# A block-sparse attention and MoE kernel with every engine's queue in the planned order

## The chip, the cores and the metric

The kernel runs on one core of a Trainium2 chip. The metric is the device time in microseconds (us) of one execution. A core has five engines with a queue each: TensorE (PE, matmuls), VectorE (DVE), ScalarE (ACT), GpSimd (POOL) and SyncE (SP, which here issues nearly all DMAs). The engines wait for each other by semaphores.

## What is computed

Attention with a block mask for 4 x 8 heads of 768 tokens by 64, then a feed-forward layer over the 3072 tokens, whose rows are the heads' outputs side by side:

```python
def _attn_ref(q, k, v, sampled_blocks):
    ...
    scores = np.where(mask, scores, -1000000000.0)
    scores = scores - np.max(scores, axis=-1, keepdims=True)
    attn = np.exp(scores)
    attn = attn / (np.sum(attn, axis=-1, keepdims=True) + 1e-09)
    return np.matmul(attn, v).astype(np.float32)

def _moe_ref(x, w_in, w_out):
    h = x @ w_in                    # 3072x512 by 512x2048
    ...
    g = np.where(pos, h, np.where(neg, 0.0, (h + beta) ** 2 / (4.0 * beta)))
    return (g @ w_out).astype(np.float32)
```

`mask` keeps the neighbouring blocks of 32, the first and last, and three sampled blocks for each row of blocks.

## The kernel before

**Precision.** Most operands are split into a rounded part (`hi`, type fp32r, cast on ACT in L196) and the remainder (`lo`, subtracted on DVE), and three products of the parts make one full product.

**A head.** q and k are loaded transposed (`qk`), cast on ACT (L196, `qkh`), and their remainder is taken by DVE (L228). DMAs on SP move the parts (L221) to the tiles KA, QA, KB and QB that the products read. Twelve max products (L267, PE) go one by one into the three `pa` banks, and DVE reduces each to a row maximum (L272). The maxima are joined (L276), turned by PE with the identity `idr` (L282, L293) and stored by ACT or DVE (L287, L298) as a row of QA, so that the score products subtract the maximum themselves. Then, for each half of the queries (`hf`) and each of six pieces of the keys: scores (L318, L319), exponential (L323, ACT), its split (L196 and L331), the sum on POOL (L338) and the product with v (L350, L351) into the one `po` bank. v is split by ACT and DVE (L243). Heads 0 to 9 (pairs 0 to 4, `WHOLE`) use unsplit values (L348) with the row sums as another column of v. Heads 0 to 7, the wide stage, use more banks and tiles for the scores.

**End of a half.** L355 (ACT) and L360 (DVE) take the result out of `po`; L373 (DVE) turns the sums, which L378 (PE) adds up. For each pair and half, L384 and L387 (DVE) take reciprocals; L397 sends them to DRAM and L399 spreads them back as `den` over 64 partitions each, both on SP; L402 (DVE) multiplies, L404 and L410 split the result into `x`. In the pairs that use unsplit values the sums themselves come to L387 by two DMAs first (L392 on ACT's queue, L393 on SP's).

**The feed-forward layer** of a batch is worked off while the next batch's heads run, in halves of 16 blocks: L472 to L474 (PE) into the bank `hp`, L478, L481 (ACT) and L484 (DVE) for the activation, its split (L196, L493), then L500 to L502 (PE). Both weight matrices are split in the kernel (conversions, L162 to L180, a chain between ACT and DVE): `moe_w_in` in the wide stage, `moe_w_out` in the next 8 heads, after which the parts of `moe_w_out` go to DRAM and are loaded again block by block (`w`, L456).

**What sets the order.** Each step is entered in a list `plan` with a planned time, by `at(t, fn, *args)`. The unit is a twelfth of a head's period (`PER = 12`). The times come from tables: `P`, `PW` (heads 0 to 7), `PA` (heads 8 to 15) and `PM` (the first half of the layer), where for example `qs` is how long before its head the cast, the moves and L228 are planned, and `vs` the same for v's split. The list is sorted by time and issued:

```python
    plan.sort(key=lambda x: x[0])
    early = [x for x in plan if x[0] < MANUAL]
    with tc.manual_schedule():
        for _, fn, args in early:
            fn(*args)
    for _, fn, args in plan[len(early):]:
        fn(*args)
```

What is issued inside `manual_schedule` stands in each engine's queue in that order. What is issued outside is a wish: the framework places the instructions of each engine by a model of its own of when they can start, with the order of issue as the priority. In the kernel before, `MANUAL` is -999 and the earliest step stands at -99, so `early` is empty. The constants (identity, mask) are planned at `TC = -90`, head 0's cast at -12.9, so in the plan the constants come first but for the first load.

Of the kernel before, what the change touches and what calls it, by code (L numbers as in the profile page):

```python
# [37 lines left out]
def body(ctx, tc, qk_t, v, sampled_blocks, moe_w_in, moe_w_out, ind, cm, negd, ident, fold, out):  # L38
# [521 lines left out]
# [3 lines that stand above are left out]
# [21 lines left out]
DELAY = 3.672  # L584
EARLY = 0
SETS = 2
MANUAL = -999
NHEADS = B * H
NMOE = B
PER = 2 * T  # L590
# [53 lines left out]
```

## Time and profile before

| | before |
|---|---|
| median of 3 runs | 981.25 us (980.53 to 983.28) |
| profiled execution | 980.94 us |
| its span | 979.0 us |
| granted PE clock, mean | 0.995 |
| PE busy | 945.3 us, 4746 matmuls |
| DVE busy | 736.8 us, 1390 instructions |
| ACT busy | 646.3 us, 1326 instructions |
| POOL busy | 251.5 us, 229 instructions |

The span runs from the first to the last instruction of the profiled execution; its time holds 1.9 us more. A row of the timeline reads: start in us, duration in us, engine, line, operation, output <- input, shapes, and in brackets how long the engine had been idle ahead of it and what released it. A row of the groups gives the count, then the busy time in us, the mean of one in ns, then the idle time ahead of the group. A row of a transfer in the chain gives when it was issued and how long until it landed. PEld is the loading of weights into PE.

### The profile page before, as it was taken

To read this page: it belongs to the slowest core of one execution; us is meant where nothing else is said; L and a number is where in the kernel's file an instruction comes from. 1 tells how busy PE (TensorE), PEld (TensorE's weight loads), DVE (VectorE), ACT (ScalarE), POOL (GpSimd) and SP (SyncE) were. 2 spreads that over 40 slices of the span, in tenths; PEclk is the share of its full clock that TensorE was granted. 3 is DMA by queue.
4 is the path that set the end of the run, shared out by engine and by line. 5 is a ranking of instruction groups with operands and counts; after the bars stand their busy time and mean duration, and the time that the engine had idled before them with its cause. 6 is when DMAs were issued, how large, how long until landed. Compare 5 with 4: busy or idle time off the path is not lost.

```text
span 979.0 us, 14671 instructions
## 1 busy us (share of the span) xinstructions
PE 945.3 (97%) x4746; PEld 833.3 (85%) x4746; DVE 736.8 (75%) x1390; ACT 646.3 (66%) x1326; POOL 251.5 (26%) x229
## 2 busy tenths in 40 slices
PE   5898999999899999999999999999999999999998
PEld 3676677888789999998999899999999999899997
DVE  5897988779998888988888888888788885422222
ACT  4686787677677676767677667776767676433433
POOL 1000000013334443433434343433434343000000
PEclk9899999999999999999999999999999999999999
DMA  6756766754364544545556453646445442433442
GB/s 193 227 155 183 200 201 214 259 173 140 129 205 144 146 148 136 178 135 154 158 154 189 118 153 120 198 138 176 137 143 178 126 114 89 154 129 129 161 129 97
DMA packets 56216, 154.44 MB, mean 158 GB/s; under 512 B 9612, under 2 KB 17952, under 8 KB 56140
## 3 DMA queue, kind: packets, MB, share of 16 engines
q1 hardware_dynamic: 56100, 153.48, 52.0%
q8 instruction: 38, 0.62, 0.3%
q14 instruction: 38, 0.31, 0.1%
q10 hardware_dynamic: 40, 0.03, 0.0%
HBM read 100.92 MB, written 14.81 MB: 118 GB/s over the span
## 4 chain that ended last, share of the span: by engine, by line
PE 88%; DVE 5%; ACT 3%; DMA 2%; issue 2%; SPq 0%; ACTq 0%; DVEq 0%
PE oa L500 8%; PE oa L502 8%; PE oa L501 8%; PE hp L472 8%; PE hp L474 8%; PE hp L473 8%; PE pa L267 7%; PE pa L318 5%; PE pa L319 5%; PE po L350 5%; PE po L348 5%; PE po L351 4%; PE oa L348 3%; DVE mc L272 1%; PE oa L318 1%
## 5 line engine op out<-in xcount | busy, mean ns | idle before, releaser
L338 POOL TENSOR_TENSOR acc<-acc,pt 128x384 f32<-128x384 f32 x176 | 202.2, 1149 | 226.2 <-ACT pt L323 190.3
L272 DVE TENSOR_REDUCE mc<-pa 128x1 f32<-128x384 f32 x384 | 202.8, 548 | 24.1 <-PE pa L267 21.0
L196 ACT CAST ph<-pt 128x384 fp32r<-128x384 f32 x264 | 135.7, 514 | 88.2 <-PE po L350 84.5
L331 DVE TENSOR_TENSOR pl<-pt,ph 128x384 fp32r<-128x384 f32 x264 | 166.3, 630 | 35.6 <-ACT ph L196 34.9
L323 ACT ACTIVATE pt<-pa 128x384 f32<-128x384 f32 x288 | 140.6, 489 | 50.8 <-PE pa L319 42.0
L472 PE MATMUL hp<-x,wi 128*128 128x384 f32 x448 | 155.0, 346 | 2.9 <-DVE r L484 2.9
L500 PE MATMUL oa<-w,gh 128*128 128x512 f32 x384 | 153.6, 400 | 0.3 <-ACT gh L196 0.3
L502 PE MATMUL oa<-w,gl 128*128 128x512 f32 x384 | 151.4, 394 | 0.0
L473 PE MATMUL hp<-x,wi 128*128 128x384 f32 x448 | 151.4, 338 | 0.0
L474 PE MATMUL hp<-x,wi 128*128 128x384 f32 x448 | 151.2, 338 | 0.0
L501 PE MATMUL oa<-w,gh 128*128 128x512 f32 x384 | 150.8, 393 | 0.0
L267 PE MATMUL pa<-KA,QA 88*128 88x384 f32 x384 | 138.8, 381 | 5.3 <-DMA QA<-qkh 3.0
L338 POOL TENSOR_TENSOR acc<-pt 128x384 f32<-128x384 f32 x44 | 45.8, 1040 | 349.4 <-ACT pt L323 349.4
L484 DVE SCALAR_TENSOR_TENSOR r<-r,hp 128x384 f32<-128x384 f32 x112 | 61.7, 551 | 74.0 <-ACT r L481 73.6
L493 DVE TENSOR_TENSOR gl<-r,gh 128x384 fp32r<-128x384 f32 x128 | 83.7, 654 | 23.4 <-ACT gh L196 22.9
L478 ACT ACTIVATE r<-hp,half_c 128x384 f32<-128x384 f32 x112 | 65.1, 582 | 53.4 <-PE hp L474 50.3
L318 PE MATMUL pa<-QA,KA 102*128 102x384 f32 x288 | 99.3, 345 | 0.8 <-ACT pt L323 0.4
L319 PE MATMUL pa<-QB,KB 128*128 128x384 f32 x288 | 97.9, 340 | 0.0
L267 PEld LDWEIGHTS pa<-KA,QA 88*128 88x128 f32 x384 | 73.2, 192 | 27.8 <-DVE mc L272 6.7
L350 PE MATMUL po<-ph,vn 128*128 128x384 f32 x264 | 91.5, 347 | 2.3 <-DVE xun L360 1.9
L472 PEld LDWEIGHTS hp<-x,wi 128*128 128x128 f32 x448 | 84.5, 189 | 8.6 <-DVE r L484 4.2
L351 PE MATMUL po<-pl,vn 128*128 128x384 f32 x264 | 88.6, 336 | 0.0
(100 smaller groups left out, 1634.1 us busy)
## 6 DMA issues: line engine op xcount, KB each, us to landing
w<-wo_dram SPq DMA_DIRECT2D x112, 512.0 KB
qk<-in_qk_t_dram SPq DMA_DIRECT2D x32, 384.0 KB
raw<-in_moe_w_in_dram SPq DMA_DIRECT2D x16, 512.0 KB
raw<-in_moe_w_out_dram SPq DMA_DIRECT2D x16, 512.0 KB
wo_dram<-w SPq DMA_DIRECT2D x16, 512.0 KB
lv<-in_v_dram SPq DMA_DIRECT2D x32, 192.0 KB
KA<-qkh SPq DMA_DIRECT2D x32, 192.0 KB
QA<-qkh SPq DMA_DIRECT2D x32, 192.0 KB
```

The lines of the kernel that those rows point to most:

```text
L267: nc.tensor.matmul(out=pm[:, 0:HALF], lhsT=QAi[0:KM, t * 128:(t + 1) * 128], rhs=KAi[0:KM, kh * HALF:(kh + 1) * HALF], start=True, stop=True)
L272: nc.vector.reduce_max(out=st["mc"][:, t, kh:kh + 1], in_=st.pop(("pm", t, kh))[:, 0:HALF], axis=AX.X)
L318: nc.tensor.matmul(out=ps[:, 0:HALF], lhsT=KAi[0:KA, ks], rhs=QAi[0:KA, cs], start=True, stop=False)
L319: nc.tensor.matmul(out=ps[:, 0:HALF], lhsT=st["KB"][:, ks], rhs=st["QB"][:, cs], start=False, stop=True)
L331: (nc.gpsimd if i < 2 * H and c in PL1 else nc.vector).tensor_tensor(out=pl, in0=st["p", c], in1=f(st["ph", c]), op=ALU.subtract)
L338: nc.gpsimd.tensor_tensor(out=st["acc", hf], in0=prev, in1=st["p", c], op=ALU.add)
L472: nc.tensor.matmul(out=hv, lhsT=wi[:, j, 0, fs], rhs=x[:, 0], start=(j == 0), stop=False)
L473: nc.tensor.matmul(out=hv, lhsT=wi[:, j, 0, fs], rhs=x[:, 1], start=False, stop=False)
L474: nc.tensor.matmul(out=hv, lhsT=wi[:, j, 1, fs], rhs=x[:, 0], start=False, stop=(j == NP - 1))
L500: nc.tensor.matmul(out=o, lhsT=gh[:, ts], rhs=w[:, 0], start=(fi == 0), stop=False)
L501: nc.tensor.matmul(out=o, lhsT=gh[:, ts], rhs=w[:, 1], start=False, stop=False)
L502: nc.tensor.matmul(out=o, lhsT=gl[:, ts], rhs=w[:, 0], start=False, stop=(fi == NF - 1))
```

## The change

One constant is changed, so that `early` holds the whole plan:

```diff
@@ -584,7 +584,7 @@
 DELAY = 3.672
 EARLY = 0
 SETS = 2
-MANUAL = -999
+MANUAL = 99999
 NHEADS = B * H
 NMOE = B
 PER = 2 * T
```

Everything is now issued inside `manual_schedule`. The instructions, tiles and transfers are the same; only their order in the queues differs. Three places:

ACT's queue at the start, before and then after. `QA_113` and `QA_114` are the two sets' QA tiles; L124 casts the mask into them, `qkh` is the cast of q and k, L247 copies v.

```order
L196 ACT_TABLE_LOAD
L196 CAST qkh<-qk 128x768
L124 CAST QA_114<-pa 24x384 x2
L247 COPY vn<-lv 128x6x64
L287 ACTIVATE QA_113<-pa 1x384
```

```order
L124 ACT_TABLE_LOAD
L124 CAST QA_114<-pa 24x384 x2
L196 CAST qkh<-qk 128x768
L287 ACTIVATE QA_113<-pa 1x384
L247 COPY vn<-lv 128x6x64
```

The mask's cast moved ahead of head 0's q and k.

DVE's queue in the wide stage, at the end of pair 1's first half, before the max products of head 5. `rc` holds the reciprocals, `den` what comes back, `cva` belongs to the conversions, `mc` takes the maxima. Before:

```order
L387 RECIPROCAL rc_876<-rc_876 24x32
L228 TENSOR_TENSOR qk_833<-qk_833,qkh_907 128x768
L180 TENSOR_TENSOR wi_119<-cva_1100,wi_119 128x512
L180 TENSOR_TENSOR wi_119<-cva_1169,wi_119 128x512
L169 TENSOR_SCALAR cva_1267<-cva_1267 128x512
L170 TENSOR_SCALAR cva_1267<-cva_1267 128x512
L172 SCALAR_TENSOR_TENSOR cva_1267<-raw_1133,cva_1267 128x512
L272 TENSOR_REDUCE mc_973<-pa_974 128x1
...
L272 TENSOR_REDUCE mc_973<-pa_1024 128x1
L402 TENSOR_TENSOR xun_698<-xun_698,den_699 128x384
```

(The line of dots stands for five more L272.) After:

```order
L228 TENSOR_TENSOR qk_832<-qk_832,qkh_906 128x768
L169 TENSOR_SCALAR cva_919<-cva_919 128x512
L170 TENSOR_SCALAR cva_919<-cva_919 128x512
L172 SCALAR_TENSOR_TENSOR cva_919<-raw_786,cva_919 128x512
L174 SCALAR_TENSOR_TENSOR cva_919<-raw_786,cva_919 128x512
L387 RECIPROCAL rc_875<-rc_875 24x32
L180 TENSOR_TENSOR wi_119<-cva_919,wi_119 128x512
L402 TENSOR_TENSOR xun_697<-xun_697,den_698 128x384
L272 TENSOR_REDUCE mc_972<-pa_973 128x1
```

Between L387 and L402 stood seven maxima, L228 and parts of three conversions; now there is one L180, and the maxima follow L402.

DVE's queue in the steady stage, at the end of the second half of an odd head (around 504 us in the profile before). `pl`, `r` and `gl` belong to the splits and the layer's activation. Before:

```order
L373 TENSOR_REDUCE psum_5646<-acc_5791 128x12
L493 TENSOR_TENSOR gl_5929<-r_5903,gh_5923 128x384
L331 TENSOR_TENSOR pl_5949<-pt_5933,ph_5947 128x384
L402 TENSOR_TENSOR xun_5482<-xun_5482,den_5863 128x384
L410 TENSOR_TENSOR x_5993<-xun_5482,x_5993 128x384
L331 TENSOR_TENSOR pl_5975<-pt_5956,ph_5971 128x384
L484 SCALAR_TENSOR_TENSOR r_5973<-r_5973,hp_5935 128x384
L331 TENSOR_TENSOR pl_6012<-pt_5981,ph_6010 128x384
L360 TENSOR_TENSOR xun_5644<-po_5847,otmp_5989 64x384
L243 TENSOR_TENSOR vn_5995<-lv_5861,vn_5995 128x6x64
```

After:

```order
L331 TENSOR_TENSOR pl_5974<-pt_5955,ph_5970 128x384
L484 SCALAR_TENSOR_TENSOR r_5972<-r_5972,hp_5934 128x384
L402 TENSOR_TENSOR xun_5481<-xun_5481,den_5862 128x384
L228 TENSOR_TENSOR qk_5842<-qk_5842,qkh_5962 128x768
L243 TENSOR_TENSOR vn_5994<-lv_5860,vn_5994 128x6x64
L360 TENSOR_TENSOR xun_5643<-po_5846,otmp_5988 64x384
L373 TENSOR_REDUCE psum_5645<-acc_5790 128x12
L331 TENSOR_TENSOR pl_6011<-pt_5980,ph_6009 128x384
```

L402, L228 and L243 moved between L484 and L360; in an even head L228 and L243 do. L373, which stood eight places ahead of L360, now follows it.

## The prediction

> **What bounds the kernel now.** I read the page's totals and chain first, then the engines' busy time by stage, then what TensorE (PE) waits for.
>
> ```profile
> span 979.0 us, 14671 instructions
> PE 945.3 (97%) x4746; PEld 833.3 (85%) x4746; DVE 736.8 (75%) x1390; ACT 646.3 (66%) x1326; POOL 251.5 (26%) x229
> PE 88%; DVE 5%; ACT 3%; DMA 2%; issue 2%; SPq 0%; ACTq 0%; DVEq 0%
> ```
>
> PE is busy 945.3 of 979.0 us and carries 88% of the chain. An order cannot shorten PE's own work, so all that a better order could win is PE's idle time, 33.7 us. The windows (us, then busy and count for PE, PEld, DVE, ACT, POOL, granted clock, DMA share, GB/s) say where that is:
>
> ```profile
> 0.00:25.00 25.00, 13.31 (x45) 9.89 (x46) 14.46 (x34) 10.39 (x19) 3.50 (x9) 1.00 0.67 193
> 25.00:160.00 135.00, 126.95 (x542) 93.64 (x542) 114.74 (x231) 98.07 (x203) 0.00 (x0) 0.96 0.67 193
> 225.00:300.00 75.00, 68.37 (x355) 60.63 (x355) 73.58 (x133) 52.70 (x112) 29.17 (x24) 1.00 0.46 151
> 300.00:840.00 540.00, 537.55 (x2827) 494.82 (x2826) 443.84 (x831) 381.88 (x797) 213.44 (x191) 1.00 0.50 147
> ```
>
> Idle are 11.7 us at the start, 8.05 in the wide stage (heads 0 to 7, here to 160 us), 6.6 between 225 and 300, where VectorE (DVE) is full (73.58 of 75), and only 2.45 in the 540 us of steady state. There PE never stops, and an order can only lose. Three of PE's waits (total, times, longest):
>
> ```profile
> PE pa L122 <- DVE KA L104: 8.7, 1, 8.7
> PE pa L267 <- DMA QA<-qkh: 3.0, 2, 2.1
> PE po L350 <- DVE xun L360: 1.9, 3, 0.9
> ```
>
> The first is the start itself, which holds in any order: nothing runs before the inputs land.
>
> **The change part by part.** No instruction, tile or transfer is added or removed, so the sum has only displaced waits. What matters is an instruction that now stands in its engine's queue ahead of others while it waits. I go by stages.
>
> **A, the start.** ACT now casts head 0's q and k as soon as they land; in the new order this cast stands behind the two mask casts (L124).
>
> ```profile
> 3.88 0.83 ACT L196 CAST qkh<-qk 128x768 fp32r<-128x768 f32 x1 [1.87 <-DMA qk<-in_qk_t_dram]
> 5.32 0.59 SPq L221 DMA_DIRECT2D QA<-qkh  x1
> 8.06 0.56 DVE L104 CAST KA<-raw 38x768 fp32r<-38x768 f32 x1 [2.90 <-DMA raw<-in_ind_dram]
> 8.68 0.83 PE L122 MATMUL pa<-KA,mb 24*24 24x384 f32 x2 [8.68 <-DVE KA L104]
> 10.04 0.21 DVE L103 CAST idr<-pt 128x128 fp32r<-128x128 f32 x1
> 10.93 0.87 ACT L124 CAST QA<-pa 24x384 fp32r<-24x384 f32 x2 [6.22 <-DVE QA L124]
> 11.61 2.93 PE L267 MATMUL pa<-KA,QA 88*128 88x384 f32 x6 [2.10 <-DMA QA<-qkh]
> 5.32 6.16 DMA QA<-qkh
> ```
>
> The mask's six small DVE steps, done now before L104, come behind it: at L103's 0.21 us each 1.3 us, an estimate. L104 ends at 8.62, the mask's matmuls follow at 9.9 and end at about 10.8, L124 ends on ACT about 12.6 (it starts 1.4 us after those matmuls' end now), the cast takes 0.83, its KA move 0.5, so QA's move is issued near 14.0 instead of 5.32. It took 6.16 us among the loads of the start, which puts the first max product (L267) at 20.2, +8.6. If it takes what a small move later takes (1.92 us, rows of part B), it starts at 16, +4.3. I take the middle, +6, and +1 because all twelve max products of head 0 now stand ahead of its first score: **+7 (4 to 10)**.
>
> **B, the wide stage.** Here each pair of heads sends its reciprocals (L387, DVE) through two transfers on SP's queue (L397 out, L399 spread back as `den`) before L402 multiplies by them.
>
> ```profile
> 101.87 0.33 DVE L387 RECIPROCAL rc<-rc 24x32 f32<-24x32 f32 x1
> 102.23 0.32 SPq L397 DMA_DIRECT2D s<-rc  x1
> 104.15 1.11 SPq L399 DMA_DIRECT2D den<-s  x2
> 109.45 0.55 DVE L402 TENSOR_TENSOR xun<-xun,den 128x384 f32<-128x384 f32 x1
> 438.26 0.33 DVE L387 RECIPROCAL rc<-rc 24x32 f32<-24x32 f32 x1
> 445.21 1.08 DVE L402 TENSOR_TENSOR xun<-xun,den 128x384 f32<-128x384 f32 x1 [0.87 <-DMA den<-s]
> ```
>
> The round trip is seen where L402 waits for it: L387 ends at 438.59, L402 is released at 445.21, 6.6 us. At 102.20 to 109.45 it is longer, but there L402 stands behind other work and waits for nothing. So the framework filled the trip: seven maxima (L272) and a conversion stand between L387 and L402. In the planned order one L180 stands there, and the maxima of the next head stand behind L402.
>
> ```profile
> L272 DVE TENSOR_REDUCE mc<-pa 128x1 f32<-128x384 f32 x384 | 202.8, 548 | 24.1 <-PE pa L267 21.0
> L267 PE MATMUL pa<-KA,QA 88*128 88x384 f32 x384 | 138.8, 381 | 5.3 <-DMA QA<-qkh 3.0 <-ACT pt L323 1.2 <-DVE mc L272 1.0
> L180 DVE TENSOR_TENSOR wi<-cva,wi 128x512 fp32r<-128x512 f32 x16 | 11.0, 686 | 4.7 <-ACT wi L196 4.6
> ```
>
> DVE then idles 6.6 - 0.7 = 5.9 us. PE goes on until the three `pa` banks are full: three max products at 0.38 and about as much of scores between them, some 2 us; the fourth max product waits, and in PE's queue everything behind it. That is 3.9 us for the first half of each of pairs 0 to 3. Behind the second half's L402 stand fewer maxima: between 0 and 3.9, I take 2. Pair 4 (heads 8 and 9), where the row also comes in by DMA and less distance is planned, gets 2 for each half. Sum 4 x 3.9 + 4 x 2 + 4 = 27.6. Against it stands what the planned order may win back, at most the 8.05 us that PE idles there now: **+20**. The lower end: L402's rows give L397 1.92 us to land (102.23 to 104.15); if `den` needed only as much behind its two issues, the trip would be 1.92 + 0.55 + 1.92 = 4.4 us, the first halves lose 1.7, the second nothing, pair 4 half, and B is +1. Upper: 3.9 in all eight halves and nothing won back, +35. I take the trip that was measured.
>
> The Trainium skill, in DMA: Bandwidth & Descriptors, section Anatomy of one DMA — SWDGE (gpsimd) path, fits a transfer as about 2.0 us plus its bytes at 436 GB/s. For L397's 3 KB that is 2.0 us, which the 1.92 us here bears out; for `den`'s 96 KB it would be 2.2, a trip of an estimated 4.2 us, and the whole sum would come out near the first rival's 1014. The 6.6 us row speaks against it: `den` shares SP's queue and the DMA engines with other loads.
>
> **C, 225 to 300 us.** DVE is full, and each of the conversions of `moe_w_out` costs it five steps.
>
> ```profile
> L169 DVE TENSOR_SCALAR cva<-cva 128x512 f32<-128x512 f32 x32 | 13.5, 421 | 4.5 <-ACT cva L168 4.1
> L170 DVE TENSOR_SCALAR cva<-cva 128x512 int32<-128x512 int32 x32 | 15.0, 472 | 0.7
> L172 DVE SCALAR_TENSOR_TENSOR cva<-raw,cva 128x512 int32<-128x512 int32 x32 | 22.8, 716 | 0.4
> L174 DVE SCALAR_TENSOR_TENSOR cva<-raw,cva 128x512 int32<-128x512 int32 x32 | 22.6, 707 | 0.3
> ```
>
> With L180 that is 3.0 us. The planned order holds conversions up to ten DVE instructions later than now, so that one to three more fall into the full stretch: 3 to 9 us more DVE work there, less what PE idles today for other reasons. **+4 (0 to 9)**.
>
> **D, steady heads 16 to 31.** On DVE the long L228 (q's and k's remainders) and L243, in odd heads also L402, now stand straight ahead of L360, which frees the one `po` bank that PE's next product needs (L350), and of L373, for which PE waits in L378. Now, the framework has them elsewhere:
>
> ```profile
> L228 DVE TENSOR_TENSOR qk<-qk,qkh 128x768 f32<-128x768 f32 x32 | 34.6, 1081 | 1.3 <-ACT qkh L196 1.2
> 503.21 0.58 ACT L478 ACTIVATE r<-hp,half_c 128x384 f32<-128x384 f32 x1
> 504.61 0.55 DVE L484 SCALAR_TENSOR_TENSOR r<-r,hp 128x384 f32<-128x384 f32 x1 [0.81 <-ACT r L481]
> 505.77 0.56 DVE L360 TENSOR_TENSOR xun<-po,otmp 64x384 f32<-64x384 f32 x1
> 506.25 0.24 PE L378 MATMUL pa<-sel,psum 128*24 128x32 f32 x2
> 506.37 0.56 DVE L243 TENSOR_TENSOR vn<-lv,vn 128x384 fp32r<-128x384 f32 x1
> 476.76 0.56 DVE L484 SCALAR_TENSOR_TENSOR r<-r,hp 128x384 f32<-128x384 f32 x1 [0.95 <-ACT r L481]
> 477.81 0.54 DVE L360 TENSOR_TENSOR xun<-po,otmp 64x384 f32<-64x384 f32 x1
> 478.47 0.38 PE L350 MATMUL po<-ph,vn 128*128 128x384 f32 x1
> ```
>
> Odd head: from L484's 504.61 on, 0.55, L402 0.55, L228 1.08, L243 0.56, L360 0.56, L373 as long as L360, 0.56: 508.47, against L378 at 506.25, 2.2 us late. Of that I take off 0.3, since L484's input can come that much earlier when ACT goes straight on from L478 (ends 503.79; L484 needs a step of about 0.55 between): +1.9. Even head: 476.76 + 0.56 + 1.08 + 0.54 + 0.54 = 479.48 against 478.47, 1.0, less 0.2: +0.8. PE has no slack in this stage to take it. 8 x 1.9 + 8 x 0.8 = **+22**; 12 if half of it finds cover in work that PE has ahead, 30 if heads 10 to 15 show it too.
>
> After the last head (840 us on) DVE is a quarter busy and nothing changes: 0. SP's queue is in planned order too, but its loads of `w` wait for a free buffer as now: 0, and if a move behind one is late, it shows in A or B.
>
> **Sum.** 7 + 20 + 4 + 22 = +53. The profiled run took 980.94 us, 1.9 more than its span, 0.3 below the median of the runs, 981.25. 981 + 53 = **1034 us**. All lower ends together give 981 + 4 + 1 + 0 + 12 = 998, all upper ones 981 + 10 + 35 + 9 + 30 = 1065.
>
> **The rivals.**
> - *The round trips are short, or hidden.* If DVE runs late enough that `den` has landed when L402's turn comes, B is between -8 (all of the 8.05 us won back) and +1, and the time 1006 to 1014. For it: DVE is busy 114.74 of 135 us there and often behind. Against: L402 waits 0.87 us even at 445.21, with much work between.
> - *Faster.* PE's waits of the first 300 us (8.05 in the wide stage, 6.6 between 225 and 300, and about 2 of the start) vanish because PE's and ACT's queues no longer carry out-of-turn work, and nothing new waits: 981 - 16 = 965. It decides if the plan places each L402 at least 6.6 us of DVE work behind its L387; by the order it has 0.7, which speaks against it.
> - *No change.* The framework's order differs in place but not in what PE waits for: 981. For it: PE's own queue is nearly the same in steady state. Against: part D's L228 and L243 now stand in the queue ahead of what PE needs.
> - *Cascade.* Each stall delays the next head's moves on SP, and PE loses 5 us in every half of every wide pair and 3 in every head: above 1066.
>
> **How the numbers follow.** The sum as worked out 0.66, short or hidden trips 0.18, cascade 0.07, faster 0.06, no change 0.03. The range 998 to 1066 holds the first two and leaves out 0.16. About 0.3% (3 us) is what a measurement of this kernel can tell from no change; faster 0.06, same 0.03, slower 0.91.
>
> **What would show it.** A: ACT's first q/k cast starts near 12.6, the first L267 near 16 to 20. B: L402 of pairs 0 to 3 shows 4 to 6 us of DVE idle released by DMA `den`, and PE waits for L272 at L267 of the same length. C: DVE still full between 225 and 300, its work there larger. D: PE's waits for L360 and L373 grow from 1.9 us to about 20 us. I am wrong if L402 finds `den` there, or if PE's loss per steady head stays under 0.5 us.

## The result and the profile after

The changed kernel takes 1128.1 us (median of 4 runs, 1123.2 to 1131.0) against 981.0 before: 1.149 times as long, 95% interval 1.146 to 1.152. The forecast was 1034 (998 to 1066). The direction was right, the size was not: 147 us were lost where 53 were expected. The profiled run took 1123.16 us with a span of 1121.3, so the two traces differ by 142.3 us, and it is this difference that is divided up below.

The page's totals and the chain after:

```profile
span 1121.3 us, 14619 instructions
PE 985.5 (88%) x4746; PEld 858.5 (77%) x4746; DVE 750.3 (67%) x1390; ACT 644.3 (57%) x1326; POOL 255.1 (23%) x229
PE 55%; DVE 7%; ACT 3%; issue 3%; POOL 1%; DMA 0%; DVEq 0%; SPq 0%; ACTq 0%; POOLq 0%
```

There are the same 4746 matmuls; but PE is now busy for 88% of the span, where it was 97%, and besides it is busy 40 us longer. Both need an explanation. The stages are cut at the first max product (L267) of heads 0, 9, 16 and 31, which starts while the head ahead of it is still at work. First come the windows of before, then those of after:

```profile
11.60:156.40 144.80, 135.83 (x570) 100.62 (x570) 121.72 (x245) 104.53 (x215) 0.00 (x0) 0.96 0.68 196
156.40:367.10 210.70, 203.20 (x1027) 177.75 (x1026) 185.21 (x338) 148.48 (x307) 61.38 (x53) 1.00 0.55 173
367.10:788.70 421.60, 419.39 (x2209) 386.31 (x2208) 353.37 (x663) 301.06 (x628) 168.44 (x150) 1.00 0.53 153
```

```profile
18.30:189.00 170.70, 141.40 (x565) 100.59 (x565) 115.22 (x226) 98.89 (x203) 0.00 (x0) 0.95 0.57 158
189.00:464.70 275.70, 223.40 (x1030) 189.72 (x1031) 202.50 (x355) 149.79 (x318) 56.88 (x54) 0.92 0.44 139
464.70:928.70 464.00, 432.79 (x2209) 398.68 (x2208) 355.98 (x662) 302.87 (x628) 175.32 (x151) 0.97 0.44 139
```

Each stage's loss is the difference of the lengths, split into PE's idle time and its longer busy time for the same products:

| stage | lost, us | PE idle | PE busy longer | forecast |
|---|---|---|---|---|
| start, to head 0's first max product | 6.7 | 6.7 | | A: 7 |
| heads 0 to 8 | 25.9 | 20.3 | 5.6 | B: 20 (pair 4's 4 us of it fall behind this cut) |
| heads 9 to 15 | 65.0 | 44.8 | 20.2 | C: 4 |
| heads 16 to 30 | 42.4 | 29.0 | 13.4 | D: 22 |
| the rest | 2.3 | | | 0 |

What PE waited for:

```profile
PE po L350 <- DVE xun L360: 27.1, 19, 5.5
PE pa L378 <- DVE psum L373: 26.1, 13, 3.9
PE pa L267 <- DVE mc L272: 24.7, 15, 3.5
PE pa L267 <- DMA QA<-qkh: 12.2, 7, 7.3
PE pa L122 <- DVE mb L118: 10.2, 1, 10.2
```

The first three rows, 77.9 of the 131 us that PE's waits come to in this view, are waits for DVE on lines that the prediction named; the last row belongs to the start. DVE itself is busy 67% of the span: it is late because of what stands ahead in its queue, not because it is full.

**Where the 40 us of busy time come from.** Short windows around one steady stall, and the product that ends it:

```profile
552.00:554.00 2.00, 2.00 (x11) 1.73 (x10) 1.29 (x4) 1.73 (x5) 0.58 (x1) 1.00 0.84 218
554.00:556.00 2.00, 0.87 (x4) 0.39 (x3) 2.00 (x2) 2.00 (x5) 0.83 (x1) 1.00 0.79 194
556.00:558.00 2.00, 0.56 (x4) 0.54 (x5) 1.96 (x5) 0.12 (x1) 0.99 (x1) 1.00 0.86 288
558.00:560.00 2.00, 2.00 (x10) 2.00 (x9) 1.41 (x4) 1.00 (x2) 0.00 (x0) 0.63 0.53 157
560.00:562.00 2.00, 2.00 (x8) 2.00 (x7) 0.80 (x2) 0.00 (x0) 1.00 (x1) 0.52 0.00 0
562.00:564.00 2.00, 2.00 (x13) 1.86 (x12) 1.54 (x3) 1.53 (x4) 0.00 (x0) 1.00 0.01 2
498.00:500.00 2.00, 2.00 (x8) 2.00 (x7) 1.32 (x3) 0.49 (x1) 1.00 (x1) 0.50 0.59 123
557.44 0.22 PE L378 MATMUL pa<-sel,psum 128*24 128x32 f32 x2 [2.57 <-DVE psum L373]
525.00:550.00 25.00, 23.63 (x126) 21.60 (x126) 20.54 (x39) 15.24 (x33) 9.06 (x9) 1.00 0.40 127
```

PE idles 2.57 us. About 1 us after it restarts, the granted clock (third column from the end) falls to 0.63 and 0.52 in these windows, that is to 0.50 for 3.4 us, so the stall costs another 1.7 us (2.0 x 0.37 + 2.0 x 0.48) when it is over. The last row is the 25 us before, with a stall of 1.37 us in it: there the clock stays at 1.00. In heads 16 to 30 all seven stalls of 2.57 us are followed so, and none of the seven of 1.37 us; but one stall of 1.40 us, at 494.22, is (the row of 498), with a second one of 0.38 us right behind it.

How much of the longer busy time this is can be read from PE's busy time inside the stretches at 0.50. In heads 16 to 30 it is 27.1 us, of which half, 13.6 us, is lost: all of the 13.4. In heads 9 to 15 it is 31.6 us, so 15.8 of the 20.2; in heads 0 to 8 it is 14.7 us against 9.5 before, so 2.6 of the 5.6. The clock makes 32 of the 39 us; where the other 7 come from is not shown. The Trainium skill, TensorE: Matmul & The Clock Gate, section Why this matters for your kernels, advises against PE-idle gaps of more than about 3 us; the trace agrees in kind, but here 2.6 us were enough each time.

### The profile page after: what moved, and what is told of

Read it like the earlier page. It is cut to its first block, busy times and chain, and to the rows that moved or that the text cites. A ratio compares the mean times of both kernels' runs of the same rounds, so it can differ in the third digit from the quotient of the medians.

```text
span 1121.3 us, 14619 instructions
## 1 busy us (share of the span) xinstructions
PE 985.5 (88%) x4746; PEld 858.5 (77%) x4746; DVE 750.3 (67%) x1390; ACT 644.3 (57%) x1326; POOL 255.1 (23%) x229
## 4 chain that ended last, share of the span: by engine, by line
PE 55%; DVE 7%; ACT 3%; issue 3%; POOL 1%; DMA 0%; DVEq 0%; SPq 0%; ACTq 0%; POOLq 0%
PE hp L472 6%; PE hp L474 6%; PE hp L473 6%; PE oa L500 6%; PE oa L502 6%; PE oa L501 6%; PE po L350 4%; PE po L351 3%; PE pa L318 3%; PE pa L267 3%; PE pa L319 3%; DVE qk L228 1%; DVE vn L243 1%; DVE xun L360 1%; ACT pt L323 1%
## 5 line engine op out<-in xcount | busy, mean ns | idle before, releaser
L338 POOL TENSOR_TENSOR acc<-acc,pt 128x384 f32<-128x384 f32 x176 | 205.8, 1169 | 312.5 <-ACT pt L323 310.3
L272 DVE TENSOR_REDUCE mc<-pa 128x1 f32<-128x384 f32 x384 | 202.3, 548 | 61.5 <-PE pa L267 59.7
L323 ACT ACTIVATE pt<-pa 128x384 f32<-128x384 f32 x288 | 139.8, 486 | 169.3 <-PE pa L319 92.6
L331 DVE TENSOR_TENSOR pl<-pt,ph 128x384 fp32r<-128x384 f32 x264 | 174.1, 659 | 85.5 <-ACT ph L196 82.2
L267 PE MATMUL pa<-KA,QA 88*128 88x384 f32 x384 | 151.5, 405 | 41.9 <-DVE mc L272 24.7
L472 PE MATMUL hp<-x,wi 128*128 128x384 f32 x448 | 160.9, 359 | 0.5 <-DVE r L484 0.5
L473 PE MATMUL hp<-x,wi 128*128 128x384 f32 x448 | 156.6, 350 | 1.5 <-DVE x L410 1.5
L474 PE MATMUL hp<-x,wi 128*128 128x384 f32 x448 | 156.8, 350 | 0.0
L267 PEld LDWEIGHTS pa<-KA,QA 88*128 88x128 f32 x384 | 78.5, 205 | 71.7 <-DVE mc L272 36.9
L350 PE MATMUL po<-ph,vn 128*128 128x384 f32 x264 | 95.2, 360 | 28.8 <-DVE xun L360 27.1
L318 PE MATMUL pa<-QA,KA 102*128 102x384 f32 x288 | 102.6, 356 | 10.5 <-DVE QA L298 4.6
L484 DVE SCALAR_TENSOR_TENSOR r<-r,hp 128x384 f32<-128x384 f32 x112 | 61.7, 551 | 71.8 <-ACT r L481 70.4
L319 PE MATMUL pa<-QB,KB 128*128 128x384 f32 x288 | 100.8, 350 | 0.0
L472 PEld LDWEIGHTS hp<-x,wi 128*128 128x128 f32 x448 | 88.9, 198 | 5.4 <-DVE r L484 1.1
L473 PEld LDWEIGHTS hp<-x,wi 128*128 128x128 f32 x448 | 88.5, 198 | 4.0 <-DVE x L410 2.0
```

The lines of the kernel that those rows point to most:

```text
L267: nc.tensor.matmul(out=pm[:, 0:HALF], lhsT=QAi[0:KM, t * 128:(t + 1) * 128], rhs=KAi[0:KM, kh * HALF:(kh + 1) * HALF], start=True, stop=True)
L272: nc.vector.reduce_max(out=st["mc"][:, t, kh:kh + 1], in_=st.pop(("pm", t, kh))[:, 0:HALF], axis=AX.X)
L323: nc.scalar.activation(out=p, in_=st.pop(("ps", c))[:, 0:HALF], func=AF.Exp, scale=SCALE)
L331: (nc.gpsimd if i < 2 * H and c in PL1 else nc.vector).tensor_tensor(out=pl, in0=st["p", c], in1=f(st["ph", c]), op=ALU.subtract)
L338: nc.gpsimd.tensor_tensor(out=st["acc", hf], in0=prev, in1=st["p", c], op=ALU.add)
L350: nc.tensor.matmul(out=po, lhsT=st["vn"][:, c], rhs=st["ph", c], start=(c == 0), stop=False)
```

## The experiments

All are the changed kernel with the edit shown, but for e14 and e15; the times stand against 1128.1 us and, for before, 981 to 983 us in each group of runs. The table gives by how much the first max product of a head comes later than in the trace of before (e13: than in e14); stages are read as differences along a row. Each row is one trace, and a stage that no edit touches differs between them: heads 0 to 8 lose 25.7 to 32.4 us, heads 9 to 15 62.6 to 68.8, heads 16 to 30 39.2 to 42.5. What lies inside these is not read as an effect.

| run | time, us | head 0 | head 9 | head 16 | head 31 | end |
|---|---|---|---|---|---|---|
| changed kernel | 1128.1 | 6.7 | 32.6 | 97.6 | 140.0 | 142.3 |
| e1 planned to time 0 | 987.8 | 6.8 | 2.5 | 2.7 | 2.9 | 3.1 |
| e2 planned to 96 | 1018.8 | 6.7 | 34.4 | 37.8 | 38.7 | 38.7 |
| e3 planned to 192 | 1083.5 | 6.3 | 33.5 | 102.3 | 105.8 | 106.2 |
| e4 steady steps moved | 1110.5 | 6.7 | 34.4 | 100.6 | 127.1 | 130.0 |
| e5 conversions later | 1136.9 | 6.3 | 33.9 | 116.6 | 159.0 | 161.0 |
| e6 lag of heads 8, 9 | 1121.0 | 6.8 | 37.3 | 96.7 | 139.2 | 140.8 |
| e7 L402 later | 1129.1 | 6.4 | 35.3 | 101.9 | 144.3 | 147.5 |
| e8 steady steps apart | 1087.7 | 6.7 | 39.1 | 101.7 | 109.4 | 111.4 |
| e9 ACT and DVE steps apart | 1121.7 | 6.3 | 29.1 | 97.7 | 136.9 | 138.3 |
| e10 conversions apart | 1119.5 | 6.1 | 23.2 | 91.6 | 133.5 | 134.9 |
| e11 first cast first | 1120.4 | 0.1 | 27.7 | 92.6 | 135.1 | 137.4 |
| e12 combined | 1070.8 | 0.5 | 16.4 | 78.8 | 85.0 | 87.9 |
| e13 against e14 | 1091.7 | 6.7 | 32.4 | 70.6 | 112.4 | 115.1 |
| e16 L360 first | 1114.6 | 6.6 | 36.0 | 89.3 | 131.2 | 133.3 |

**Which stage loses.** Three kernels in which the planned order holds only up to a time:

```diff
-MANUAL = 99999
+MANUAL = 0      # e1; 96 in e2, 192 in e3
```

> Only what is planned before time 0 (constants, preparation of head 0 and part of head 1) is in planned order; the framework orders the rest. Stage theory (each stretch of the program makes its own loss): the loss of the start alone, 6.7 us by the shift of head 0's first max product between the two traces, so about 988 us. Rival (the start's loss is made good later, since the framework fills behind it): within 2 us of before, 981 to 983.

> Planned order up to time 96, that is through the wide stage (heads 0 to 7), the framework after that. Stage theory: the shift of head 9's first max product between the two traces, 33 us, so 1011 to 1016 us. Rival (carry-over: later losses are the aftermath of queues upset in the wide stage): well over that, 1050 or more, since the aftermath remains.

> Planned order up to time 192, that is through heads 8 to 15 with the conversions of the second weight matrix, the framework after that. Stage theory: the shift of head 16's first max product, 98 us, so 1075 to 1085 us. Rival (the steady heads lose because the queues come out of the conversions upset): near the changed kernel, 1115 to 1130.

987.8 (ratio 1.006, 1.003 to 1.009), 1018.8 (1.039, 1.036 to 1.041) and 1083.5 us (1.105, 1.101 to 1.109): as the stage theory said, e2 a little above it. Once the framework takes over, little more is lost: in e2 head 31 is 38.7 us late, where head 9 was 34.4 late. Each stage makes its own loss; the carry-over falls. The other rows bear this out from the other side: heads 16 to 30 lose 39 to 42.5 us in every row that leaves them alone, whatever was lost ahead of them. In e1's profiled run (984.0 us, among the shorter of ten from 983.4 to 993.6) about 4 of the start's 6.8 us are won back in the wide stage; the median is 5.8 us above before, so most runs win back less.

**The start.** e11 plans head 0's cast ahead of the constants:

```diff
-        at(pre - G["qs"] - 0.4, hi)
+        at(-91 if i == 0 else pre - G["qs"] - 0.4, hi)
```

> All in planned order, but head 0's cast of q and k is planned ahead of the constants, so that it stands first in ACT's queue. Theory (term A: the cast stands behind the mask's casts): the first max product starts near 12 to 14 us and not at 18.3, and 4 to 7 us are won, 1121 to 1124. Rival (the moves on SP stand behind the constants' loads, or the lost time is made good elsewhere): under 2 us.

1120.4 us, 7.7 less, a little more than expected, and head 0's first max product is where it was before (0.1 us late). So term A's cause is shown: the cast's place behind the mask's casts. The rows of the changed kernel:

```profile
11.47 1.28 ACT L124 ACT_TABLE_LOAD   x1 [11.47 <-DVE QA L124]
12.76 0.84 ACT L124 CAST QA<-pa 24x384 fp32r<-24x384 f32 x2
13.62 0.83 ACT L196 CAST qkh<-qk 128x768 fp32r<-128x768 f32 x1
15.06 0.59 SPq L221 DMA_DIRECT2D QA<-qkh  x1
18.30 2.93 PE L267 MATMUL pa<-KA,QA 88*128 88x384 f32 x6 [7.26 <-DMA QA<-qkh]
```

**The steady heads.** The changed kernel at the end of a half of an even head:

```profile
523.97 0.95 DVE L228 TENSOR_TENSOR qk<-qk,qkh 128x768 f32<-128x768 f32 x1
524.84 1.36 DVE L243 TENSOR_TENSOR vn<-lv,vn 128x384 fp32r<-128x384 f32 x1
526.13 0.54 DVE L360 TENSOR_TENSOR xun<-po,otmp 64x384 f32<-64x384 f32 x1
526.82 0.41 PE L350 MATMUL po<-ph,vn 128*128 128x384 f32 x1 [1.37 <-DVE xun L360]
```

This is the order of term D, and PE stands for it: 1.37 us in each even head and, with L402 ahead as well, 2.57 us in each odd one. The prediction had 0.8 and 1.9. The difference is the length of L228 and L243: they were priced at 1.08 and 0.56 us, 1.64 together, and take 2.31 here and 2.32 in the odd head, while a sum on POOL runs beside them (last section):

```profile
553.87 1.77 DVE L228 TENSOR_TENSOR qk<-qk,qkh 128x768 f32<-128x768 f32 x1
555.57 0.55 DVE L243 TENSOR_TENSOR vn<-lv,vn 128x384 fp32r<-128x384 f32 x1
```

e4 moves these steps just behind L360 and L373; e8 moves them apart, to where DVE idled. The casts, loads and moves that are planned with them move too.

```diff
-P = {... 'qs': 9.647, ... 'vs': 9.131, ... 'xm': 0.774, 'xh': 1.0, ...}
+P = {... 'lo': 0.8, ... 'vs': 8.75, ... 'xm': 1.3, 'xh': 1.5, ...}     # e4; L228 at -qs + lo
+P = {... 'qs': 10.85, ... 'vs': -0.6, ...}   # e8; xm, xh + 0.53 in heads 16 to 31 but for j = 3
```

> All in planned order as in the changed kernel, but for heads 16 to 31 the planned times of L402 (xm 0.774 to 1.3, with its cast xh 1.0 to 1.5), of L228 (0.4 units later) and of v's split L243 (vs 9.131 to 8.75) are moved just behind L360 and L373. Theory (these three stand ahead of what frees PE): PE's waits for L360 and L373 after 465 us (31 us) go, and with them the clock dips behind them; 35 to 45 us faster than the changed kernel, 1083 to 1093. Rival (DVE is late in the steady heads for other reasons, such as L484 waiting for ACT): under 10 us faster, over 1118.

> All in planned order, but for heads 16 to 31: q and k prepared 1.2 units earlier (qs 10.85), v's split only when its head begins (vs -0.6), L402 0.53 units later except in each batch's last pair. So L228, L243 and L402 stand apart from each other and from L360, where DVE idled. Theory (e4 removed the waits for L360 and L373, but moved 2.5 us of DVE work in one piece ahead of L331, L493 and the maxima): 33 to 45 us faster than the changed kernel, 1083 to 1095. Rival (the planned order leaves other waits in the steady heads): no better than e4, 1105 to 1112.

e4 takes 1110.5 us, half of the gain expected: after 465 us PE's waits for L360 and L373 fall from 30.7 to 5.5 us, but DVE then has L360, L373, L402, L228 and L243 in one piece, and 11.9 us of waits for the maxima behind it (L272) appear. e8 takes 1087.7 us, as expected; heads 16 to 30 lose 7.7 us instead of 42.4. In e8 after 465 us little is left of the waits (19.9 us stood in the first row in the changed kernel, 10.8 in the last):

```profile
PE pa L378 <- DVE psum L373: 3.6, 9, 1.1
PE pa L267 <- DVE mc L272: 2.0, 6, 0.3
PE po L350 <- DVE xun L360: 1.9, 3, 0.8
```

So term D's mechanism is shown: three instructions of DVE with the steps tied to them, and where they stand.

**The wide stage.** The changed kernel's wait on a round trip:

```profile
104.44 0.33 DVE L387 RECIPROCAL rc<-rc 24x32 f32<-24x32 f32 x1
109.53 0.56 DVE L402 TENSOR_TENSOR xun<-xun,den 128x384 f32<-128x384 f32 x1 [3.62 <-DMA den<-s]
```

```diff
-XLATE = 2.0
+XLATE = 4.0
```

> All in planned order, but L402 and what follows it are planned 2 units later in pairs 0 to 2 (XLATE 2 to 4), behind maxima of the next head. Theory (term B: the round trip of the reciprocals stands ahead of the maxima): DVE's waits for den in the wide stage (10.6 us in 4 waits) go and most of PE's waits for L272 (19.2 us): 10 to 18 us faster than the changed kernel, 1110 to 1118. Rival (in the wide stage the conversions of the first matrix hold up DVE, which waits 13.0 us at L169 for ACT): under 5 us faster.

1129.1 us: nothing, as the rival had it. No wait of DVE for `den` is left in the wide stage, yet PE's wait for the maxima there, 19.2 us in the changed kernel, stays (first row, of e7), and other waits of DVE have grown in its place (second and third, 13.0 and 9.4 us in the changed kernel):

```profile
PE pa L267 <- DVE mc L272: 20.3, 13, 2.8
DVE cva L169 <- ACT cva L168: 16.5, 12, 4.8
DVE qk L228 <- ACT qkh L196: 13.2, 5, 3.6
```

Term B was about right in size, by luck, and wrong in its cause, or at least had one of several. e9 and e10 take the next of these away: the ACT and DVE steps of a conversion are planned 0.8 units apart (e9), and its DVE steps also 0.4 apart from each other (e10).

```diff
-            at(t, bits)
-            at(t + P["cs"], split)
+            at(t - 0.8, bits)            # L168 alone
+            at(t, bits1)                 # L169, L170
+            at(t + 0.4, bits2)           # L172; + 0 in e9
+            at(t + 0.8, bits3)           # L174; + 0 in e9
+            at(t + P["cs"], split)       # the cast
+            at(t + P["cs"] + 0.8, split_lo)
```

> All in planned order; the conversions' ACT and DVE steps, which share one planned time in the changed kernel, are planned apart: L168 (ACT) 0.8 units before the four DVE steps, the cast L196 0.8 units before L180. Theory (a DVE step planned at the same time as the ACT step it needs stands at the head of DVE's queue and waits, with all behind it): DVE's waits at L169 for L168 (23.3 us) and at L180 for the cast (8.7 us) mostly go, PE's waits for L272 and L360 before 465 us fall, 12 to 30 us faster than the changed kernel, 1098 to 1116. Rival (the length of the DVE block and not its wait is what PE sees): under 6 us faster.

> As e9, and the four DVE steps of a conversion are planned 0.4 units apart (L169 with L170, L172, L174) and no longer back to back, so that other DVE work can stand between. Theory of the wait alone: within 4 us of e9. Rival (the block of 2.3 us ahead of L360 or a maximum is the loss): 8 to 25 us faster than e9.

1121.7 and 1119.5 us. e9's 6.4 us less are under what its theory asked for, although DVE's waits at L169 before 470 us fell from 23.3 to 3.7 us: this wait of DVE for ACT cost PE little. e10 is 2.2 us below e9, within the 4 us in which the two were to agree. By its trace the gain of e10, 9.4 us at head 9 (23.2 against 32.6), lies in the wide stage; heads 9 to 15 lose as much as ever.

**Heads 9 to 15**, where nearly all of the error lies. The changed kernel at the end of a half:

```profile
297.04 1.37 DVE L172 SCALAR_TENSOR_TENSOR cva<-raw,cva 128x512 int32<-128x512 int32 x1
298.44 0.69 DVE L174 SCALAR_TENSOR_TENSOR cva<-raw,cva 128x512 int32<-128x512 int32 x1
299.06 0.57 DVE L373 TRANSPOSE_TENSOR_REDUCE psum<-acc 128x12 f32<-128x384 f32 x1
299.55 0.51 DVE L360 TENSOR_TENSOR xun<-po,otmp 64x384 f32<-64x384 f32 x1
300.20 0.66 PE L350 MATMUL po<-ph,vn 128*128 128x384 f32 x1 [4.18 <-DVE xun L360]
```

The conversion's steps stand ahead of L373 and L360, as L228 and L243 do later. The plan has it so wherever both occur: the conversions of the second matrix come every 3 units at -0.02 (modulo 3), L373 at 0.04, L360 at 0.31. But these conversions are planned from 98.98 to 143.98, so they fill heads 8 to 11 and not eight heads, and heads 8 and 9 have no L360 and L373. It is so at the ends of three halves, and each is a long stall of PE: 4.18 us in the rows above, and

```profile
323.00 0.66 PE L350 MATMUL po<-ph,vn 128*128 128x384 f32 x1 [5.47 <-DVE xun L360]
345.13 0.30 PE L378 MATMUL pa<-sel,psum 128*24 128x32 f32 x2 [3.86 <-DVE psum L373]
```

In all that is 13.5 of the 44.8 us by which PE's idle time grew in this stage. e5 moves the conversions behind (and the loads of both matrices one unit later); e6 lets ACT stop waiting for the three `pt` buffers in heads 8 and 9.

```diff
-P = {... 'cl': 9.0, ... 'co': 5.196, ...}
+P = {... 'cl': 8.0, ... 'co': 4.796, ...}                                   # e5
-... {**P, **PA} if i < 2 * H else P
+... {**P, **PA, **({"lag": 2.9} if whole else {})} if i < 2 * H else P      # e6
```

> All in planned order, but the conversions of the second weight matrix are planned 0.4 units later (co 5.196 to 4.796), so that their five DVE steps (3 us) stand behind L373 and L360 and not straight ahead of them, and their loads one unit later (cl 9 to 8), so that SP's queue does not stand at a load until the buffer is free. Theory (position of the conversions): of PE's waits for L360 and L373 between 189 and 465 us, 21.4 us, most go, with the clock dips behind them: 20 to 35 us faster than the changed kernel, 1093 to 1108. Rival (the stretch is simply full of DVE work, as the prediction had it): the waits reappear elsewhere, under 10 us faster.

> All in planned order, but in heads 8 and 9 (unsplit values, three buffers for the exponentials) the values are planned 2.9 instead of 3.5 units behind their scores, so that an exponential no longer stands in ACT's queue ahead of the product that frees its buffer. Theory: ACT's waits of L323 for L348 (37.8 us in 21 waits between 189 and 465 us) hold back what stands behind them on ACT, and the 24 us that heads 8 and 9 lost come largely from it: 12 to 22 us faster than the changed kernel, 1106 to 1116. Rival (ACT's idle is off the path and the loss is SP's and DVE's): within 4 us of it.

e5 takes 1136.9 us (ratio to before 1.157, 1.155 to 1.159): slower, and the expected gain did not come. PE's waits for L360 and L373 between 189 and 472 us did fall from 21.4 to 8.9 us, but other losses rose by more: 43.7 us are lost between the first max products of heads 9 and 11, where the changed kernel loses 25.7. Its ACT and DVE rows point to the reason (37.8 and 3.0 us stood here in the changed kernel):

```profile
ACT pt L323 <- PE po L348: 53.9, 22, 6.0
DVE w L180 <- ACT w L196: 33.9, 11, 6.4
```

A reading of these rows, not tested by itself: the cast of a conversion now stands in ACT's queue behind an exponential that waits for its buffer, L180 waits for the cast at the head of DVE's queue, and the maxima wait behind L180. e6 takes 1121.0 us, 7.1 less where 12 to 22 were expected: ACT's waits of 37.8 us for L348 are gone, but ACT's waits for L319 rise from 48 to 72 us. In its trace heads 9 to 15 lose 5.6 us less and heads 0 to 8 4.7 us more. e5 and e6 together were not run, apart from what e12 joins. Whether the conversions matter at all was told by leaving out their steps L169 to L174 for the second matrix, in both orders; such a kernel does not compute the layer:

```diff
-            nc.scalar.activation(out=f(a), in_=f(hi32), func=AF.Abs)
+            if nc.scalar.activation(out=f(a), in_=f(hi32), func=AF.Abs) and done: return
```

> Planned order; the four DVE steps L169 to L174 are left out of the conversions of the second matrix (so its values are not those of the reference; 16 x 2.3 = 37 us of DVE work fall away between 160 and 465 us), ACT's L168, the cast and L180 remain. To be read against e14. Theory (conversion steps standing as a block ahead of what frees PE make the loss of heads 9 to 15): the loss of that stretch against the framework's order of the same program falls from 65 to 30 us or less, and the difference e13 - e14 of the whole time from 147 to about 110 or less. Rival (the head's own chain between ACT and DVE makes it, whatever DVE's load): the difference stays at 130 or more.

> The same omission of L169 to L174 for the second matrix in the framework's order of the kernel before. If PE bounds that stretch there, as its 203 busy of 211 us say: 975 to 981 us. If DVE's 73.6 of 75 us between 225 and 300 us bound it: 5 to 8 us faster, 973 to 976.

1091.7 and 976.0 us (ratio to before 0.995, 0.993 to 0.997). The whole difference falls from 147 to 115.7 us, the loss of heads 9 to 15 from 65.0 to 38.2: most of the way to what the theory asked for (110 and 30). So the conversions' DVE steps make 27 us of it, and more by their place than by their load, since the framework's order loses only 5 us to the same steps. About 18 of the 27 fall between the first max products of heads 11 and 13, where the three stalls are (25.2 us lost there in the changed kernel, 6.9 in e13); how the other 9, in heads 9 and 10, come about was not followed up. For the rest, e16 plans L360 ahead of L373 and the row of maxima earlier:

```diff
-PA = {... 'mw': 0.515, ... 'oa': 0.814, ...}
+PA = {... 'mw': 0.9, ... 'oa': 0.45, ...}
```

> Planned order; in heads 8 to 15 L360 is planned ahead of L373 (oa 0.814 to 0.45) and the row of maxima L298 0.385 units earlier (mw 0.515 to 0.9). Theory (what is left of term C is the order of small steps around the end of a half, as in term D): PE's waits between 326 and 465 us for L360 (6.7), L373 (5.1) and L298 (4.6) halve, 6 to 12 us faster than the changed kernel, 1116 to 1122. Rival (DVE comes to that place late whatever the order of the small steps): under 4 us.

1114.6 us, 13.5 less, more than expected: heads 9 to 15 lose 53.3. Between 326 and 465 us PE's wait for L298 (4.6 us) is gone and that for L360 falls from 6.7 to 3.5, while that for L373 doubles to 10.4. Beyond this what is left of the 38 us is not settled; the largest single piece of it lies between the first max products of heads 9 and 10 (11 us even without the conversions).

**All together, and the same plan under the framework.** e12 joins e6, e7, e8, e11 and e10 (0.7 units apart), with L228 0.4 to 0.6 units later in heads 0 to 15; e15 is e12 with the framework's order (`MANUAL = -999`).

> All in planned order with the changes of e6, e7, e8, e11 and of e10 (DVE steps 0.7 units apart here) together, and L228 planned 0.4 to 0.6 units later in heads 0 to 15. If the losses are separate, the gains add: 40 (e8), 7 (e6), 4 to 7 (e11), 12 to 30 (e9, e10): 1045 to 1065. If a wait taken from one place only moves in the full stretch before 465 us: 1065 to 1085. Below 982 would be a version better than both; not expected.

> The edits of e12 to the planned times, but ordered by the framework as in the kernel before. Theory (the framework repairs what a planned time has wrong, so that the table hardly matters to it): within 1.5% of before, 975 to 996 us. Rival (the table's times are tuned to the framework, and each moved step costs there too): 1000 us or more. Under 978 it would be a version better than both.

e12 takes 1070.8 us (ratio 1.090, 1.086 to 1.095), the second of the two cases: 57 of 147 us are mended, 62 us remain in heads 9 to 15. The gains of e8, e10 and e11 are there together (heads 0 to 8 lose 15.9 us, heads 16 to 30 lose 6.2); that of e6 is not. e15 takes 979.7 us (0.999, 0.997 to 1.000): the moved times, worth 57 us in the planned order, are worth nothing measurable under the framework. No kernel here is measurably faster than before, apart from e14, which computes less.

## Why the prediction was wrong

- **What bounds:** right in part. PE was the bound, and 94 of the 142 us are PE idle behind the start, most of it waiting for DVE. But "An order cannot shorten PE's own work" was taken to mean that PE's busy time stays as it is, and it grew by 40 us.
- **A, +7:** 6.7 by the trace, 7.7 by e11. The way there was a little different. By the prediction's own rows L124 would have ended at 13.1 and not at 12.6 (10.8 + 1.4 + 0.87); it ended at 13.6, with ACT's table load, done at 0.73 before, now at 11.47 behind the wait, 1.28 us long. QA's move took 3.2 us (15.06 to 18.3), between the bounds.
- **B, +20:** 25.9, of which 20.3 are idle time. The size is luck. The waits of DVE for `den` exist, but in this stage they are 1.9, 3.6, 1.0 and 4.1 us, not 5.9 in the first half of each pair, and taking them away brought nothing (e7). Nor did the planned order win anything back against them: PE's idle time there rose from 9.0 to 29.3 us. The trips at whose end L402 waits took 4.6 to 7.7 us, so the 6.6 taken was within what happens; three of the six, such as the 4.8 us of the row shown (104.77 to 109.53), are nearer to the short rival's 4.4 us. The prediction's estimate of 4.2 us by the Trainium skill (DMA: Bandwidth & Descriptors, section Anatomy of one DMA — SWDGE (gpsimd) path) is under all six. What holds PE in this stage is only in part known: spreading the conversions (e10) gave some 9 us, and the other waits of DVE on ACT were not priced.
- **C, +4, the step that failed:** 65.0, which is 61 of the 89 us that the sum is short of the traces' difference. The term priced only the *amount* of DVE work that falls into the full stretch, 3 to 9 us, and left out where a conversion stands in DVE's queue. The runs show 44.8 us of idle PE and 20.2 us of longer busy time in its place. The conversions make 27 us (e13 against e14); the three stalls in which one stands ahead of L373 and L360, 13.5 us, are the reasoning of D, which was not applied to them. The cause of the other 38 us stays open: e16 takes 12 of the 65 away by reordering small steps, 7 of them between the first max products of heads 13 and 16, where no conversion is left; e6, e9 and e10 change little here.
- **D, +22:** mechanism right, size too small, 42.4. PE's idle time grew by 29.0 us, since L228 and L243 take 0.7 us longer in each head than priced; 13.4 more came from the clock.
- **The clock, the second step that failed, put at nothing in the sum:** 32 us over the three stages, 29 of them in the two where the mean clock fell from 1.00. A stall's price is its length only if it is short.
- **The rivals:** the cascade (7%) came nearest in time, and the steady heads did lose 2.8 us each, near its 3. But e2 and e3 show that nothing cascades: each stage loses by itself.

## What to carry to other kernels

In an engine's queue of fixed order, count what stands between an instruction's inputs and the instruction itself, for each one that frees a bank or buffer of the bounding engine; every long step planned just ahead of one is a stall per repetition. Price such a step with what runs beside it on POOL. In the wide stage and in heads 9 to 15, removing one wait mostly showed the next (e5, e6, e7, e9); only where the steps could be moved to idle time of DVE did nearly all of the loss go (e8). This plan's times serve well only as priorities for a scheduler that moves work past a wait (e12 against e15). Price a TensorE stall of 2.5 us or more with the slow clock that follows it.

## What the runs showed of the hardware

- The granted clock fell to half for 3.4 us after each of the seven stalls of 2.57 us in heads 16 to 30, after none of the seven of 1.37 us, and after the one of 1.40 us (rows above). Where between them it begins is not shown.
- DVE and POOL hold each other up: L243 took 1.36 us at 524.84 where the prediction's row has 0.56, beside this sum on POOL, which takes about 1.0 us alone and ended at 525.79. L243 ended 0.4 us after it. In the odd head it is L228 that is longer, 1.77 us at 553.87, beside a sum from 553.42 to 554.83.

```profile
523.99 1.80 POOL L338 TENSOR_TENSOR acc<-acc,pt 128x384 f32<-128x384 f32 x1 [1.95 <-ACT pt L323]
```

The Trainium skill, SBUF — State Buffer, section SBUF: two separate sides, says that a DVE instruction with two SBUF inputs and a GpSimd instruction that reads SBUF exclude each other for the whole instruction; the rows agree.
